# Attention with a forget gate, then a GELU feed-forward layer: another decay and another order in batches 0 and 1

## The chip, the cores and the metric

The kernel runs on one core of one Trainium2 chip. A core has five engines that run their own queues of instructions and wait for each other through semaphores: TensorE (PE in the profile; its weight loads are listed as PEld), VectorE (DVE), ScalarE (ACT), GpSimd (POOL) and SyncE (SP), which only issues transfers. Transfers issued by SP and by POOL go to two different queues, but the same 16 DMA engines carry both. The metric is the device time of one execution in microseconds (us); less is better.

## The reference

There are 8 batches of 8 heads, a sequence of 576 and a head size of 64. `f` is a forget gate between 0.8 and 1. Per head, and then for all 4608 tokens:

```python
scores = scale * np.matmul(q, k.transpose(0, 1, 3, 2))
log_f = np.log(np.clip(f, 0.0001, 1.0))
cum = np.cumsum(log_f, axis=-1)
decay = cum[:, :, :, None] - cum[:, :, None, :]
causal = np.triu(np.ones((S, S), dtype=bool), k=1)
scores = np.where(causal, -1000000000.0, scores + decay)
attn = softmax of scores over the last axis
out = np.matmul(attn, v)
...
x = out of all heads side by side, (4608, 512)
h = x @ w_in                      # 512 -> 2048
y = gelu(h) @ w_out               # 2048 -> 512
```

The decay of query t and key s is the sum of log f over s+1 to t. Whatever depends on the query alone falls out of the softmax, so a key needs only a weight that is proportional to exp(-cum[s]). Up to a factor per head that is also the product of f over all positions after s.

## The kernel before, in words

**Layout.** A head pair i (0 to 3) has its queries and keys transposed in `qT[i]` and `kT[i]`, 64 rows for each of its two heads. The 576 keys are five blocks of 128 (`K0`; the last overlaps the fourth and its first 64 rows are zero). The score tiles of a pair are packed into four tiles t (`STILES`), each with both heads, and `scores` makes one: matmuls into a bank pair `s` (two such buffers), then one exponential on ACT into an `e` tile. The causal mask is either added before the exponential by small matmuls of `after` and `key_of` (where `on_pe` is true), or applied after it by an `affine_select` on POOL (L312). The tiles t=1 use four fixed buffers `e4` whose first 64 columns have to stay zero.

**Weights of the keys.** `wT` holds the key weights of all 64 heads, transposed by TensorE. `weigh_v` multiplies v by them (L269; on VectorE for the first two pairs of batch 0, else on POOL) and from batch 1 on copies the weights themselves beside v (L276), so that `attend` gets numerator and denominator in one run of 15 matmuls a head (L331). `normalize` divides (L344, L345), and the result is transposed into `xT`.

**Feed-forward.** `gemm1` computes 16 blocks of the hidden layer for 512 tokens of a batch (L386), each followed by a GELU on ACT (L406). The remaining 64 tokens of each batch are collected in `tails` by `x_tail` and done at the end. The second GEMM of a batch runs as fill between the attention tiles of the next batch: a generator gives one step at a time and `take(fill, n)` runs n of them. A step "n" is one matmul over 128 rows, a step "r" two matmuls over 64 rows each into two banks, which VectorE adds up.

**Batches 0 to 2.** `first_attention` (batch 0) runs while data are still arriving. `second_attention` (batch 1) has only 16 fill steps, `gemm2_first`: for two of the four row blocks, over the first half of `w_out` (L518). The rest of batch 0's second GEMM is `gemm2_second` (L542) and `PLAN_0`, run in batch 2 together with batch 1's (`gemm2_third`; `FILL_2` says how many steps follow each tile). From batch 2 on all is one pattern (`attention`).

**What sets the order.** The order is written by hand: an engine runs its instructions in the order of the program, and SP's and POOL's transfers are issued in that order too. The order of transfers is kept by small instructions on POOL: `gate` and `behind` (L568, L573) read one element of a tile, so that POOL waits there until that tile has landed, and a `memset` of a column of `v_sb` that the load will overwrite (L152, L623, L797) makes SP's next load wait for POOL. POOL issues q, k, `w_in` and `w_out` (L108, L172, L176); SP issues f, v (L120, five transfers a call), the transposing transfers of q and k from batch 2 on (L236, two halves of the heads, q and k each) and of x (L370), and the outputs. From batch 2 on `untangle` (L250, VectorE) sorts the transposed q and k into `qT` and `kT`; batches 0 and 1 have them transposed by TensorE (`transposes_first`, L208 and L217 to L222).

**PSUM.** Three pools of two buffers: `s` (two banks each), `o` and `m` (one bank each). A tile taken from a pool waits until the tile before it in that buffer has been read.

Of the kernel before, what the change touches and what calls it, by code (L numbers as in the profile page):

```python
# [9 lines left out]
FP32 = mybir.dt.float32  # L10
# [43 lines left out]
def kernel(  # L54
# [100 lines left out]
    e4 = [consts.tile([P, 2, 448], BF16, name=f"e4{i}") for i in range(4)]  # L155
    for t in e4:
        nc.gpsimd.memset(t[:, :, 0:D], 0.0)
    diagonal(ident_fp, Alu.not_equal, 1.0, 0)
    load_qk_tokens(0, 6, 8)
# [20 lines left out]
    ones = consts.tile([BH, S], FP32)  # L180
    lf = f_sb
    cum = consts.tile([BH, S], FP32)
    wk = f_sb
    nc.vector.memset(ones, 1.0)
    nc.vector.memset(wT[0:D, 4, :], 0.0)
    nc.vector.tensor_scalar(f_sb, f_sb, 1e-4, 1.0, Alu.max, Alu.min)
    nc.scalar.activation(lf, f_sb, Act.Ln)
    nc.vector.memset(v_sb[0:D, :, 4, :], 0.0)
    nc.vector.tensor_tensor_scan(cum, ones, lf, 0.0, Alu.mult, Alu.add)
    spark = consts.tile([1, 1], FP32)  # L190
    nc.scalar.activation(spark, ones[0:1, 0:1], Act.Exp)

    def warm_up(n):

        ps = m_psum.tile([P, TC], FP32, tag="m", name="ps_w")
        for _ in range(n):
            nc.tensor.matmul(ps, warm[:, 0:P], warm, start=True, stop=True)
# [82 lines left out]
    def scores(b, i, t):  # L280
        on_pe = b == 0 or (b == 1 and i == 0)
# [170 lines left out]
    PLAN_0 = [(2, "o", 16 * "r"), (3, "m", 14 * "r" + 2 * "n")]  # L452
# [57 lines left out]
    def gemm2_first(c):  # L510

        pss = [
            m_psum.tile([P, d_model], FP32, tag="m", name="ps2") for _ in range(2)
        ]
        for kq in (0, 4):
            for ts in range(2):
                for kt in range(kq, kq + 4):
                    nc.tensor.matmul(  # L518
                        pss[ts],
# [3 lines left out]
                        stop=(kt == 7),  # L523
                    )
                    if kt == 7:
                        ot_of.append(
                            o_pool.tile([P, d_model], FP32, tag="ot", name="ot")
                        )
                        copy = nc.scalar.copy if ts else nc.vector.tensor_copy
                        copy(ot_of[ts], pss[ts])  # L530
                    yield

    def gemm2_second(c):

        for ts, pool, tag in ((0, o_psum, "o"), (1, m_psum, "m")):
# [3 lines left out]
            for kt in range(8, n_ff):  # L539
                for r in range(2):  # L540
                    rows = slice(r * D, (r + 1) * D)
# [4 lines left out]
                        start=(kt == 8),  # L546
                        stop=(kt == n_ff - 1),
                    )
                if kt == n_ff - 1:
                    nc.vector.tensor_tensor(ot_of[ts], ot_of[ts], banks[1], Alu.add)  # L550
                    sum_out(c, ts, ot_of[ts], banks[0])
                yield

    def gemm2_third():
        yield from gemm2_second(0)
        yield from gemm2_rows(0, PLAN_0)
# [18 lines left out]
    def first_attention():  # L575
# [6 lines left out]
        def attend_head(i, h):  # L582
# [5 lines left out]
        nc.scalar.activation(  # L588
            wk, cum, Act.Exp, bias=cum[:, S // 2 : S // 2 + 1], scale=-1.0
        )  # L590
        warm_up(2)
        scores(0, 0, 0)
        scores(0, 0, 1)
        transposes(1, m_psum, "m")
        scores(0, 0, 2)
        psw = o_psum.tile([P, NBLK, BH], FP32, tag="o", name="psw")
        for n in range(NBLK):
            nc.tensor.transpose(
                psw[:, n, :], wk[:, K0[n] : K0[n] + P], ident_fp[:BH, :BH]
# [24 lines left out]
        load_v(1, 0, 4)  # L624
# [6 lines left out]
        for i, t in ((2, 2), (2, 3), (3, 0), (3, 1), (3, 2), (3, 3)):  # L631
            scores(0, i, t)
            attend_head(*heads.pop(0))
# [87 lines left out]
    def second_attention():  # L721
# [23 lines left out]
        transposes(1, o_psum, "o")  # L745
        transposes(2, m_psum, "m")
        transposes(3, o_psum, "o")
        tiles(0, 2)
# [4 lines left out]
        take(fill, 4)  # L753
        weigh_v(1, 2)
# [12 lines left out]
        behind(qk_of[2][1], H - 1)  # L767
        load_w_out(2)
        load_w_out(3)
        run(2)  # L770
        take(fill, 4)
# [74 lines left out]
```

## Time and profile before

| | us |
|---|---|
| median of 5 executions | 338.3 |
| all five | 337.43, 338.23, 338.3, 339.55, 339.72 |
| the profiled execution | 339.55 |
| its span, first to last instruction | 337.6 |
| TensorE busy in it | 328.5 |
| VectorE, ScalarE, GpSimd busy | 181.1, 209.3, 122.2 |
| first attend of batch 0 starts at | 17.0 |
| first GEMM of batch 0 starts at | 25.3 |
| first scores of batch 1 at | 40.9 |
| first scores of batch 2 at | 72.3 |

All times inside the kernel are counted from the start of the span. A line of the timeline or of the groups reads: start and length in us, engine, line of the kernel, operation, the tile written and the tiles read (buffer numbers left out), their shapes, how many instructions are put together, and in brackets how long the engine had been idle before and what ended that. L12 is line 12 of the kernel. "SPq" is a transfer that SP issues; its length is the time of the issue, not of the transfer. The named releaser of a wait is inferred; when the one that is named had long been done, it was another, often a transfer.

### The profile page before, as it was taken

The numbers are of one execution on the slowest core, as the hardware profiler recorded it, in microseconds if no ns is written. First come the engines' busy times: TensorE is split into PE (matmuls) and PEld (weight loads), VectorE is DVE, ScalarE is ACT, GpSimd is POOL, SyncE is SP. The second block draws the span as 40 slices with busy tenths as digits, with TensorE's granted clock in tenths as the row PEclk, the third lists the DMA queues.
The fourth block names the chain that finished last, engine by engine and source line by source line (L and its number), as shares of the span: only waits on it lengthen the run. The fifth ranks groups of instructions, "written<-read, shape, count | busy, mean of one in ns | idle before, by whom it ended". The sixth has DMA issues, their size and how long they took to land.

```text
span 337.6 us, 7820 instructions
## 1 busy us (share of the span) xinstructions
PE 328.5 (97%) x3161; PEld 173.6 (51%) x3161; DVE 181.1 (54%) x414; ACT 209.3 (62%) x299; POOL 122.2 (36%) x250
## 2 busy tenths in 40 slices
PE   8799989999999999999999999999999999999995
PEld 3584455445554456545554465446544654444443
DVE  4661166674556944895479547974696540020011
ACT  6957698673553689278927982788468855404600
POOL 8091088009536135533454254624351420000000
PEclk9979999999999999999999999999999999999999
DMA  7999999996998989697968697679810241011013
GB/s 115 178 142 185 196 196 163 133 201 127 229 211 186 139 156 208 124 140 114 212 163 123 119 208 176 95 121 208 142 62 2 81 61 64 0 63 64 0 39 86
DMA packets 104627, 44.16 MB, mean 131 GB/s; under 512 B 83408, under 2 KB 100048, under 8 KB 104592
## 3 DMA queue, kind: packets, MB, share of 16 engines
q1 hardware_dynamic: 87296, 29.52, 45.7%
q0 software_dynamic: 16896, 13.63, 27.9%
q8 instruction: 24, 0.39, 0.5%
q10 hardware_dynamic: 400, 0.52, 0.4%
q14 instruction: 11, 0.09, 0.1%
HBM read 36.85 MB, written 9.44 MB: 137 GB/s over the span
## 4 chain that ended last, share of the span: by engine, by line
PE 91%; DMA 2%; POOL 1%; DVE 1%; issue 1%; ACT 1%; SPq 0%; POOLq 0%; ACTq 0%; DVEq 0%
PE ps L386 37%; PE ps L482 27%; PE o L331 10%; PE ps L422 8%; PE s L300 7%; DMA v_sb<-in_v_dram 2%; ACT e L310 1%; PE ps L542 1%; POOL q L108 1%; PE ps_x L364 1%; PE ps L518 1%; SPq L120 0%; POOL k L108 0%; DVE qT L217 0%; DVE kT L217 0%
## 5 line engine op out<-in xcount | busy, mean ns | idle before, releaser
L406 ACT ACTIVATE g<-ps 128x512 bf16<-128x512 f32 x144 | 82.1, 601 | 83.6 <-PE ps L386 83.6
L310 ACT ACTIVATE e<-s 128x896 bf16<-128x896 f32 (+2 forms) x128 | 100.3, 835 | 23.1 <-PE s L300 16.8
L386 PE MATMUL ps<-xT,w_in_sb 128*128 128x512 bf16 x512 | 112.5, 379 | 0.0
L482 PE MATMUL ps<-w_out_sb,g 64*128 64x512 bf16 (+1 forms) x711 | 108.3, 377 | 0.0
L386 PEld LDWEIGHTS <-w_in_sb 128*128 128x128 bf16 x576 | 56.0, 98 | 67.5 <-issue 1.8
L312 POOL TENSOR_SCALAR_AFFINE_SELECT e<-e 128x256 bf16<-128x256 bf16 (+1 forms) x135 | 49.1, 383 | 87.9 <-ACT e L310 87.5
L482 PEld LDWEIGHTS <-g 64*128 64x128 bf16 (+1 forms) x711 | 40.5, 95 | 34.3 <-issue 4.5
L269 POOL TENSOR_TENSOR vw<-v_sb,wT 128x640 bf16<-128x640 f32 x30 | 38.5, 1286 | 28.5 <-PE ps L542 15.9
L300 PE MATMUL s<-qT,kT 64*128 64x320 bf16 (+4 forms) x384 | 44.8, 278 | 2.5 <-ACT e L310 1.4
L250 DVE COPY kT<-tk 64x288 bf16<-64x288 bf16 x96 | 45.0, 469 | 1.6
L250 DVE COPY qT<-tq 64x288 bf16<-64x288 bf16 x96 | 37.6, 392 | 5.6 <-DMA tq<-q 4.2
L331 PEld LDWEIGHTS <-e 128*128 128x128 bf16 x960 | 35.2, 99 | 9.5 <-issue 2.8
L331 PE MATMUL o<-vw,e 128*128 128x65 bf16 x960 | 38.2, 196 | 1.3 <-DVE vw L269 1.3
L490 DVE COPY ot<-ps 128x512 f32<-128x512 f32 x20 | 13.8, 692 | 47.2 <-PE ps L482 47.2
L345 DVE TENSOR_TENSOR x<-o,r 128x320 bf16<-128x320 f32 x64 | 31.5, 491 | 2.3
L300 PEld LDWEIGHTS <-kT 64*128 64x128 bf16 x384 | 20.2, 94 | 24.1 <-issue 7.9
L431 DVE COPY ot<-ps 128x512 f32<-128x512 f32 (+2 forms) x9 | 5.7, 632 | 49.6 <-PE ps L422 49.6
L422 PE MATMUL ps<-w_out_sb,g 128*128 128x512 bf16 (+2 forms) x144 | 28.0, 355 | 0.0
L422 PEld LDWEIGHTS <-g 128*128 128x128 bf16 x144 | 13.5, 98 | 14.5
L344 DVE RECIPROCAL r<-o 128x5 f32<-128x5 f32 x64 | 12.1, 189 | 13.4 <-PE o L331 13.3
L502 DVE TENSOR_TENSOR ot<-ot,ps 128x512 f32<-128x512 f32 x22 | 15.1, 685 | 1.1
L386 PE MATMUL ps<-tails,w_in_sb 128*128 128x512 bf16 x64 | 14.3, 377 | 0.0
(69 smaller groups left out, 139.1 us busy)
## 6 DMA issues: line engine op xcount, KB each, us to landing
out_dram<-ot SPq DMA_DIRECT2D x32, 256.0 KB, 2.6
v_sb<-in_v_dram SPq DMA_DIRECT2D x24, 256.0 KB, 4.9
q<-in_q_dram POOLq DMA_DIRECT2D x6, 576.0 KB, 6.4
k<-in_k_dram POOLq DMA_DIRECT2D x6, 576.0 KB, 8.9
v_sb<-in_v_dram SPq DMA_DIRECT2D x22, 128.0 KB, 5.4
w_in_sb<-in_moe_w_in_dram POOLq DMA_DIRECT2D x4, 512.0 KB, 7.7
w_out_sb<-in_moe_w_out_dram POOLq DMA_DIRECT2D x4, 512.0 KB, 10.6
q<-in_q_dram POOLq DMA_DIRECT2D x4, 144.0 KB, 4.7
```

The source lines that it names most:

```text
L250: nc.vector.tensor_copy(rows[:, odd], src[odd * D : (odd + 1) * D, 2 * i + h].rearrange("d j p -> d p j"),)
L269: eng.tensor_tensor(vw(b)[:, hs, :, 0:D], v_sb[:, hs, :, :], w.unsqueeze(3).to_broadcast([P, 2, NBLK, D]), Alu.mult,)
L300: nc.tensor.matmul(to, *ab, start=half < 0, stop=half == 1 or not masked)
L310: nc.scalar.activation(et[:, :, z:c], st[:, :, z:c], Act.Exp, scale=scale)
L312: nc.gpsimd.affine_select(out=et[:, :, c0 + z : c0 + P], in_=et[:, :, c0 + z : c0 + P], compare_op=Alu.is_ge, fill=0.0, base=z, pattern=[[ ...
L331: nc.tensor.matmul(o[:, m, :], e_of[b, i, t][:, h, c : c + P], vw_of[b][:, 2 * i + h, n, :], start=(n == 0), stop=(n == m),)
L345: nc.vector.tensor_tensor(x_of[b, i][:, :, h, :], o[:, :, 0:D], r.unsqueeze(2).to_broadcast([P, NBLK, D]), Alu.mult,)
L386: nc.tensor.matmul(ps, w_in_sb[:, kt, ffb * P : (ffb + 1) * P], src[:, kt, 0:TC], start=(kt == 0), stop=(kt == n_dm - 1),)
L406: nc.scalar.activation(g_of[c][ffb], ps, Act.Gelu)
L422: nc.tensor.matmul(pss[ts][:, c0:c1], g_of[c][kt][:, ts * P : (ts + 1) * P], w_out_sb[:, kt, c0:c1], start=(kt == 0), stop=(kt == n_ff - 1),)
L482: nc.tensor.matmul(banks[r], g_of[c][kt][rows, ts * P : (ts + 1) * P], w_out_sb[rows, kt, :], start=kt == (steps.index("r") if r else 0), ...
L502: nc.vector.tensor_tensor(ot, ot, bank, Alu.add)
```

## The change

The key weights come from a product: `tensor_tensor_scan` on VectorE runs backwards over f, multiplies from 2^80 on, and adds zeros (`none`). The logarithm, the cumulative sum and the exponential of it are gone. The scan stands after the copies of the first pair's keys. The `e4` tiles are zeroed by VectorE and not by POOL, the last loads of q and k of batch 0 come before the mask of `ident_fp`, the second warm-up is two matmuls of 256 columns and not of 512, and the key transposes of pair 1 come after score tile (0, 2).

In batch 0 the last six score tiles are made in twos, followed by two heads' `attend`. In batch 1 pair 3 is masked by TensorE. v of batch 1 arrives in three lots (two, two and four heads), the last two behind the gate on q of batch 1. `gemm2_first` does all four row blocks over the first quarter of `w_out`, and `gemm2_second` all four over the rest. The second quarter of `w_out` is loaded together with the third and fourth, behind the gate on k of batch 2; k of batch 2 is issued later than q, in the middle of batch 1's attention. The fill steps of batch 1 stand at other places.

```diff
-    e4 = [consts.tile([P, 2, 448], BF16, name=f"e4{i}") for i in range(4)]
-    for t in e4:
-        nc.gpsimd.memset(t[:, :, 0:D], 0.0)
+    load_qk_tokens(0, 6, 8)
     diagonal(ident_fp, Alu.not_equal, 1.0, 0)
-    load_qk_tokens(0, 6, 8)
...
-    nc.vector.memset(ones, 1.0)
+    nc.vector.memset(none, 0.0)
+    nc.scalar.activation(spark, none[0:1, 0:1], Act.Exp)
+    nc.vector.memset(v_sb[0:D, :, 4, :], 0.0)
     nc.vector.memset(wT[0:D, 4, :], 0.0)
+    nc.vector.memset(decay[:, S - 1 : S], 2.0**80)
+    e4 = [consts.tile([P, 2, 448], BF16, name=f"e4{i}") for i in range(4)]
+    for t in e4:
+        nc.vector.memset(t[:, :, 0:D], 0.0)
     nc.vector.tensor_scalar(f_sb, f_sb, 1e-4, 1.0, Alu.max, Alu.min)
-    nc.scalar.activation(lf, f_sb, Act.Ln)
-    nc.vector.memset(v_sb[0:D, :, 4, :], 0.0)
-    nc.vector.tensor_tensor_scan(cum, ones, lf, 0.0, Alu.mult, Alu.add)
-    nc.scalar.activation(spark, ones[0:1, 0:1], Act.Exp)
...
-        on_pe = b == 0 or (b == 1 and i == 0)
+        on_pe = b == 0 or (b == 1 and i in (0, HP - 1))
...
-    PLAN_0 = [(2, "o", 16 * "r"), (3, "m", 14 * "r" + 2 * "n")]
...
     def gemm2_first(c):
-        for kq in (0, 4):
-            for ts in range(2):
-                for kt in range(kq, kq + 4):
+        for two in (0, 2):
+            pss = [
+                m_psum.tile([P, d_model], FP32, tag="m", name="ps2") for _ in range(2)
+            ]
+            for ts in (two, two + 1):
+                for kt in range(n_ff // 4):
...
-                        copy = nc.scalar.copy if ts else nc.vector.tensor_copy
+                        copy = nc.scalar.copy if ts == 3 else nc.vector.tensor_copy
...
     def gemm2_second(c):
-        for ts, pool, tag in ((0, o_psum, "o"), (1, m_psum, "m")):
+        kts = range(n_ff // 4, n_ff)
+        for ts in range(n_sub):
+            pool, tag = ((o_psum, "o"), (m_psum, "m"))[ts % 2]
+            steps = "r" * len(kts) if ts < 3 else "r" * (len(kts) - 2) + "nn"
...
     def gemm2_third():
         yield from gemm2_second(0)
-        yield from gemm2_rows(0, PLAN_0)
         yield from gemm2_rows(1, PLAN_1)
...
         transposes(0, o_psum, "o")
-        nc.scalar.activation(
-            wk, cum, Act.Exp, bias=cum[:, S // 2 : S // 2 + 1], scale=-1.0
+        nc.vector.tensor_tensor_scan(
+            decay[:, S - 2 :: -1],
+            f_sb[:, S - 1 : 0 : -1],
+            none[:, 0 : S - 1],
+            2.0**80,
+            Alu.mult,
+            Alu.add,
         )
-        warm_up(2)
+        warm_up(2, 2 * P)
         scores(0, 0, 0)
         scores(0, 0, 1)
-        transposes(1, m_psum, "m")
+        transposes_first(0, 1, 0, m_psum, "m")
         scores(0, 0, 2)
+        transposes_first(0, 1, 1, m_psum, "m")
...
-        load_v(1, 0, 4)
+        load_v(1, 0, 2)
...
-        for i, t in ((2, 2), (2, 3), (3, 0), (3, 1), (3, 2), (3, 3)):
+        for i, t in ((2, 2), (3, 0), (3, 2)):
             scores(0, i, t)
+            scores(0, i, t + 1)
+            attend_head(*heads.pop(0))
             attend_head(*heads.pop(0))
...
         tiles(0, 0)
-        transposes(1, o_psum, "o")
-        transposes(2, m_psum, "m")
+        transposes(1, m_psum, "m")
+        transposes(2, o_psum, "o")
+        take(fill, 2)
+        tiles(0, 2)
         transposes(3, o_psum, "o")
-        tiles(0, 2)
         take(fill, 2)
         tiles(1, 0)
         run(0)
         tiles(1, 2)
         take(fill, 4)
+        load_qk_tokens(2, which="k")
         weigh_v(1, 2)
...
         behind(qk_of[2][1], H - 1)
+        load_w_out(1)
         load_w_out(2)
         load_w_out(3)
         run(2)
-        take(fill, 4)
+        take(fill, 2)
         av(3, 0)
...
                 if ffb == 12:
                     behind(qk_of[1][0], H - 1)
-                    nc.gpsimd.memset(v_sb[:, 4:8, 0, 0:1], 0.0)
+                    nc.gpsimd.memset(v_sb[:, 2:8, 0, 0:1], 0.0)
+                    load_v(1, 2, 4)
                     load_v(1, 4, 8)
                     weigh_v(1, 0)
-                    load_w_out(1)
                     weigh_v(1, 1)
-                    load_qk_tokens(2)
+                    load_qk_tokens(2, which="q")
```

## The prediction

> **What bounds the kernel now.** I read the page first, for the shares.
>
> ```profile
> span 337.6 us, 7820 instructions
> PE 328.5 (97%) x3161; PEld 173.6 (51%) x3161; DVE 181.1 (54%) x414; ACT 209.3 (62%) x299; POOL 122.2 (36%) x250
> PEclk9979999999999999999999999999999999999999
> ```
>
> TensorE is busy nearly all the time, so a part of the change is worth only what it does to TensorE's few holes. The slice line shows one stretch of reduced clock past the start. The table of windows gives it (columns: length; busy time of PE, weight loads, DVE, ACT, POOL; granted clock; DMA share; GB/s):
>
> ```profile
> 10.24:13.66 3.42, 2.69 (x66) 1.96 (x66) 1.93 (x5) 3.36 (x6) 0.00 (x0) 1.00 1.19 216
> 13.66:17.07 3.41, 1.70 (x39) 1.24 (x38) 2.43 (x4) 3.01 (x4) 0.89 (x2) 1.00 0.58 126
> 17.07:20.48 3.41, 3.41 (x53) 2.75 (x53) 2.02 (x5) 0.83 (x2) 3.35 (x4) 0.50 0.62 86
> ```
>
> A window with TensorE 50% busy was followed by half clock, one with 79% was not. Next, the timeline of batch 0:
>
> ```profile
> 16.16 1.56 DVE L269 TENSOR_TENSOR vw<-v_sb,wT 128x640 bf16<-128x640 f32 x2 [0.75 <-DMA v_sb<-in_v_dram]
> 17.04 0.98 PE L331 MATMUL o<-vw,e 128*128 128x65 bf16 x15 [1.35 <-DVE vw L269]
> 18.60 0.70 ACT L310 ACTIVATE e<-s 128x640 bf16<-128x640 f32 x1 [1.91 <-PE s L300]
> ```
>
> The first attend waits for v from HBM, not for the decay, and the scores queued behind it leave ACT idle too. Then the timeline where batch 2 starts, with the queue entries that feed it:
>
> ```profile
> 49.34 0.41 POOL L312 TENSOR_SCALAR_AFFINE_SELECT e<-e 128x256 bf16<-128x256 bf16 x1 [0.19 <-ACT e L310]
> 49.97 1.28 POOL L269 TENSOR_TENSOR vw<-v_sb,wT 128x640 bf16<-128x640 f32 x1 [0.22 <-POOL e L312]
> ...
> 56.50 0.18 POOL L573 CAST gate<-k 96x1 f32<-96x1 bf16 x1
> 56.63 1.56 POOL L176 DMA_DIRECT2D w_out_sb<-in_moe_w_out_dram  x2
> ...
> 75.71 0.69 DVE L502 TENSOR_TENSOR ot<-ot,ps 128x512 f32<-128x512 f32 x1
> ...
> 76.25 1.28 POOL L269 TENSOR_TENSOR vw<-v_sb,wT 128x640 bf16<-128x640 f32 x1 [15.89 <-PE ps L542]
> ...
> 80.61 1.72 POOL L312 TENSOR_SCALAR_AFFINE_SELECT e<-e 128x256 bf16<-128x256 bf16 x5
> ...
> 83.95 1.11 PE L331 MATMUL o<-vw,e 128*128 128x65 bf16 x30
> ```
>
> POOL's 15.89 us is put down to a matmul, but the last v load of batch 2 was issued at 71.36 and took 4.7 us, so it landed at 76.1: v is what POOL waited for. From there POOL works without a gap (two weighings, the q and k issues of batch 3, five masks) until 82.33. The attend that needs the masks starts at 83.95, so v has 1.6 us of slack there. The transfers around it, software queue (q0) and SP's queue (q1), are packets, MB and share, in the stretches 60 to 64, 64 to 68 and 70 to 75 us:
>
> ```profile
> q0 software_dynamic: 348, 0.36, 87.2%
> q1 hardware_dynamic: 224, 0.06, 46.7%
> ...
> q0 software_dynamic: 619, 0.62, 91.1%
> q1 hardware_dynamic: 623, 0.16, 30.7%
> ...
> q1 hardware_dynamic: 4468, 1.13, 134.0%
> ```
>
> While w_out loads, SP's queue gets 156 packets per us (623/4); alone it gets 894 (4468/5). The transposes of q and k and the loads of v for batch 2 all stand in SP's queue behind this.
>
> **The change part by part.**
>
> *Decay and start.* Gone are Ln (0.68 us on ACT), the Exp of the decay (0.77) and one table load (1.28). The scan (1.35, DVE) now runs after the key copy, about 7.1 to 8.4, ahead of the next query copy at 8.51; its reversed reading has no row. Between 1.35 and twice that, the worst delays a key copy by 1.3 us, which the 1.35 us wait for v absorbs. I take 0. ACT's exponentials start 0.1 us earlier, and the first attend still waits for v. The four e4 memsets (0.22 each on POOL; the DVE memset of a similar size took 0.17) go into DVE's idle time before f lands at 3.6. The last q and k loads are issued 0.8 us sooner and share the transfers with v: v lands between 0.3 earlier and 0.3 later; 0. The two smaller warm-up matmuls lie ahead of a copy that TensorE waits for anyway: 0. The later key transposes leave the copy ready at about 10.4, when ACT frees the score bank (10.5): 0, or 0.2 if late.
>
> *Tiles in twos.* Scores (2,3), 0.54 us at half clock (17.95 on), move into the 1.35 us hole. Scores (3,1) now fall into the half-clock window instead and cost 0.3 more. Net -0.25. If the extra 0.45 us (50% to 63% busy) keeps the clock up, the 3.3 us of half-clock work that follows takes about 1.9: another -1.4. The window lies between the two rows above; it is nearer to the throttled one, so I take -0.25. The Trainium skill ("TensorE: Matmul & The Clock Gate", the table of why this matters) warns of idle gaps over about 3 us. This trace throttled after a longest gap of 1.35 us, so the measurement decides; by the rule the clock would play no part and the head would gain 0.25 in any case.
>
> *Batch 1.* The 16 plus 94 matmuls of the early second GEMM are only reordered; VectorE gets two more copies of 0.68, in idle time. Two fill steps (0.43) move from the tail to the front. There they lie beside ACT's stream, which has 0.2 to 0.3 us holes; ACT gains 0.2 and loses as much. Pair 3 gets 18 mask matmuls: a masked and a plain (t=3) tile took 0.33 and 0.32 us, while the mask rows' busy time gives 1.9 per pair (9.5 over five pairs); I take 0.4, since the work is narrow and overlaps. POOL is spared 1.9 us of selects (4 at 0.41, one at 0.29). But the k issue (0.78) now stands between mask (1,3) and weighing (1,2), so the masks of pair 2 end at 55.3 instead of 54.5 and `run(2)`, at 54.79 before, waits until then. With the two fills gone from behind it, the stage ends 0.1 later; bounds -0.4 and +0.6. v in three lots: half of 2304 packets leaves the queue before 39, q and k of batch 1 land 1 to 2 us sooner, and the rest of v lands by about 45 (47 before). w_out's first quarter (43.96 before) lands by about 42.5, just in time for a fill at 42.8. If it lands as before, the fill holds the scores up 1.1, of which ACT's own backlog hides half.
>
> *w_out's second quarter, and k of batch 2.* Its 512 KB leave 43 to 49 and join the other two behind the gate on k. They are 512 packets (619 packets were 0.62 MB); at 155 per us the shared stretch grows 3.3 us. In it q1 still moves 515 packets, worth 0.6 us alone: +2.7 on what stands last, v. k itself is issued at 49.8 (46.13 before, landing 55.8). From the issue, 1.6 us of start, 768 packets at 249 per us alone (1745 in 47 to 54) or 156 beside the q transposes, and 1.5 us to the landing give 56.0 to 57.8; I take 57.1, the middle. The gate opens at 57.1 and not 56.5: +0.6. So v lands 3.3 later, 79.4; POOL's 6.25 us from landing to last mask end at 85.7; the attend moves from 83.95 to about 85.75: **+1.8**. Bounds on v's delay: 1.5 (w_out at the 207 per us that w_in had alone in 20 to 23 us, gate as early as before), which the slack hides, cost 0; and 6.0 (k at 57.8 and one more pause like 62 to 63.5 us), cost +4.4. Beside it, VectorE: the last k transpose is 2 to 3 us later, `untangle` ends near 78, and its two adds (0.69 each) free the o banks at 79.3. The third row block needs them at 78.4, since the first two are 12 steps long now, not 8. That 0.9 us lies inside the 1.8. The last w_out quarter lands at 69.3 + 3.9 = 73.2 and is read at 74.3.
>
> The Trainium skill ("SBUF — State Buffer", the warning on DVE blocking DMA in the section "SBUF: two separate sides") says that VectorE's fast copies keep GpSimd from writing descriptors. Here the q issue at 107.47 took 0.81 us beside such copies, as elsewhere. By the page the third w_out issue, at 58.7, could wait out copies of 0.34 from 59.8, an estimate of under 0.5; by the row, nothing.
>
> **The sum.** The late v sets a time of its own: the small gains ahead (-0.25 + 0.1) only lengthen the wait for it. So +1.8 on the profiled execution's own 339.55 us (span 337.6 and 1.95 around it): 341.35. That execution lies 1.25 above the median; on the median 338.3 it is 340.1. After 84 us TensorE has no hole to give it back.
>
> **The rivals.**
> *The slack holds* (338.2). The transfers have time: the sum of all loads is unchanged, and q0 moved only 33 packets in 56 to 60. Then v is at most 1.6 us late and -0.25 + 0.1 is left. Against it: 60 to 75 us has no room.
> *The clock stays full* (336.4), the other side. Place: 17 to 20.5 us; price -1.4 - 0.25, and -0.3 from batch 1 near its bound. It decides when the window before it is busy enough, somewhere between 50% and 79%, and v of batch 2 keeps its slack because POOL's masks, the k issue and the gate move up with TensorE. Against it: several loads before 44 us run at their own pace.
> *w_out lands last* (343). If the mixed traffic pauses as in 60 to 64 (572 packets against 1242), the last quarter lands at 75 to 77 and TensorE stops at its twelfth step in front of everything else. 1.1 us of slack speaks against it.
> *The product decay changes nothing*: it is off the path whichever rival holds.
>
> **How the numbers follow.** Late v 0.50 (own range 339.3 to 342.2), slack holds 0.23, full clock 0.23, w_out last 0.04. Half a per cent, 1.7 us, is about what a measurement can tell. Of late v 0.07 stays below 340.0, so same is 0.23 + 0.07 = 0.30, slower 0.43 + 0.04 = 0.47, faster 0.23. The range 336.2 to 342.2 takes in the fast case's centre and late v's upper half, and leaves out about 0.1 on either side.
>
> **What would show it.** Right: POOL's first weighing of batch 2 at 79 or later and the first batch 2 attend waiting on POOL; three w_out issues from about 57; ACT without its 1.91 us hole at 16.7. Wrong: that weighing before 78, or no half clock after 17 us. The prediction fails most easily on the pace of the mixed queues, for which there is one stretch of evidence.

## The result: 0.44% slower, and lost in another place than forecast

The changed kernel takes 339.54 us (median of 43 executions) against 338.13 (80 executions of the kernel before): a ratio of 1.0044, 95% interval 1.0031 to 1.0057. The forecast was 340.1 against 338.3. The profiled execution took 340.64 us with a span of 338.7, 1.1 above its median.

Some executions of every kernel here run a few microseconds at a reduced TensorE clock and most of them are 1 to 5 us longer, so where I compare spans below I take those whose mean granted clock was 0.997 or more ("at full clock"): a median of 335.7 for the kernel before (29 of 35 that ran beside the first experiments) and of 337.6 after (37 of all 44).

The head of the page, after:

```profile
span 338.7 us, 7859 instructions
PE 327.8 (97%) x3179; PEld 171.4 (51%) x3179; DVE 183.1 (54%) x421; ACT 206.9 (61%) x296; POOL 119.6 (35%) x241
PEclk9999999999999999999999999999999999999999
```

The shares hardly move: 18 matmuls more, POOL 2.6 us less, and no slice below full clock. The windows that answer to the three shown of before:

```profile
10.24:13.66 3.42, 2.78 (x68) 1.95 (x67) 2.45 (x6) 3.31 (x6) 0.00 (x0) 1.00 1.22 231
13.66:17.07 3.41, 2.80 (x68) 2.15 (x68) 3.10 (x5) 3.38 (x5) 1.63 (x3) 1.00 0.65 136
17.07:20.48 3.41, 3.33 (x88) 2.73 (x86) 2.44 (x8) 2.79 (x5) 2.37 (x3) 1.00 1.08 138
```

One would like to credit the change with the full clock after 17 us. A second profile of the unchanged kernel takes that away; its windows there:

```profile
13.66:17.07 3.41, 2.57 (x59) 1.92 (x59) 3.19 (x6) 2.93 (x4) 1.92 (x4) 1.00 0.62 106
17.07:20.48 3.41, 3.41 (x88) 2.78 (x86) 2.50 (x7) 2.87 (x4) 3.41 (x5) 1.00 1.07 177
```

So the half clock was a chance of the one execution that the forecast was read from (mean clock 0.995). From here on "before" in a comparison of times within the span is this second profile (span 336.0). The start after, in the timeline:

```profile
15.32 1.55 DVE L268 TENSOR_TENSOR vw<-v_sb,wT 128x640 bf16<-128x640 f32 x2
...
16.27 1.12 PE L330 MATMUL o<-vw,e 128*128 128x65 bf16 x30
...
17.90 1.62 ACT L309 ACTIVATE e<-s 128x896 bf16<-128x896 f32 x2 [0.61 <-PE s L299]
```

The 1.35 us hole of TensorE and ACT's 1.91 are not there. But most of both belonged to that one execution as well; in the second profile of before they are 0.51 and 0.50:

```profile
16.12 0.63 PE L331 MATMUL o<-vw,e 128*128 128x65 bf16 x15 [0.51 <-DVE vw L269]
```

The first GEMM of batch 0 starts at 22.75, against 23.08: 0.33 gained. Then batch 1, TensorE and ACT:

```profile
42.15 0.60 PE L516 MATMUL ps<-w_out_sb,g 128*128 128x512 bf16 x2 [1.97 <-DMA w_out_sb<-in_moe_w_out_dram]
43.23 1.51 ACT L309 ACTIVATE e<-s 128x896 bf16<-128x896 f32 x2 [1.48 <-PE s L299]
```

The same wait before, second profile:

```profile
42.89 0.39 PE L518 MATMUL ps<-w_out_sb,g 128*128 128x512 bf16 x1 [0.51 <-DMA w_out_sb<-in_moe_w_out_dram]
```

The early fill step waits 1.97 us for w_out's first quarter, and the score tiles queued behind it starve ACT for 1.48. The first GEMM of batch 1 starts at 56.65, against 55.88. POOL's line of work after:

```profile
55.20 0.18 POOL L575 CAST gate<-k 96x1 f32<-96x1 bf16 x1 [1.41 <-DMA k<-in_k_dram]
55.43 2.32 POOL L173 DMA_DIRECT2D w_out_sb<-in_moe_w_out_dram  x3
...
77.07 1.28 POOL L268 TENSOR_TENSOR vw<-v_sb,wT 128x640 bf16<-128x640 f32 x1 [17.91 <-PE ps L544]
...
79.81 0.84 POOL L108 DMA_DIRECT2D q<-in_q_dram  x1
```

and before, second profile:

```profile
55.43 1.57 POOL L176 DMA_DIRECT2D w_out_sb<-in_moe_w_out_dram  x2
73.41 1.28 POOL L269 TENSOR_TENSOR vw<-v_sb,wT 128x640 bf16<-128x640 f32 x1 [15.02 <-DMA v_sb<-in_v_dram]
...
76.16 0.84 POOL L108 DMA_DIRECT2D q<-in_q_dram  x1
```

The gate is passed at 55.2 in both and the issues behind it begin at the same 55.43, three in place of two, and v of batch 2 is weighed 3.66 us later; q and k of batch 3, which stand behind that weighing on POOL, are issued 3.65 later. Why v is late shows in the queues in the stretch of 64 to 68 us (packets, MB, share), after:

```profile
q0 software_dynamic: 624, 0.62, 91.4%
q1 hardware_dynamic: 624, 0.16, 29.9%
```

The same stretch before, second profile:

```profile
q1 hardware_dynamic: 2978, 0.75, 96.9%
q0 software_dynamic: 209, 0.20, 29.2%
```

With w_out under way SP's queue gets 156 packets per us (624/4), one for each packet of the software queue; before, w_out was nearly done by then. The attend of batch 2 pays for this only 0.5: its two heads start at 82.57 and 83.52, against 81.81 and 82.28. The larger price comes 20 us later. TensorE at the first GEMM of batch 2:

```profile
102.98 1.06 PE L385 MATMUL ps<-xT,w_in_sb 128*128 128x512 bf16 x4
105.27 2.97 PE L385 MATMUL ps<-xT,w_in_sb 128*128 128x512 bf16 x13 [1.22 <-DMA xT<-x]
```

and before, second profile, where it runs through:

```profile
101.75 6.42 PE L386 MATMUL ps<-xT,w_in_sb 128*128 128x512 bf16 x29
```

What it waits for, the last transposes of x, come late out of SP's queue. SP's queue in the timeline after:

```profile
86.67 8.11 SPq L120 DMA_DIRECT2D v_sb<-in_v_dram  x5
...
102.58 2.56 SPq L369 DMA_TRANSPOSE xT<-x  x2
```

The same two steps before, second profile:

```profile
85.70 5.03 SPq L120 DMA_DIRECT2D v_sb<-in_v_dram  x5
...
97.78 2.55 SPq L370 DMA_TRANSPOSE xT<-x  x2
```

SP spends 8.1 us on the issues of v for batch 3, not 5.0, while q and k of batch 3 are loading: k lands at 92.25 (11.6 us after its issue), and before at 86.06 (9.1), when SP had only begun. The x transposes stand behind these issues. Milestone by milestone, after less before: scores of batch 1 −0.28; first GEMM of batch 1 +0.77; scores of batch 2 +0.76; second attend head of batch 2 +1.24; scores of batch 3 +2.65; end +2.7. That is one profile against one; at full clock the medians differ by 1.9, the profiled execution after being one of the longer ones.

### The profile page after: what moved, and what is told of

Read it like the earlier page. It is cut to its first block, busy times and chain, and to the rows that moved or that the text cites. A ratio compares the mean times of both kernels' runs of the same rounds, so it can differ in the third digit from the quotient of the medians.

```text
span 338.7 us, 7859 instructions
## 1 busy us (share of the span) xinstructions
PE 327.8 (97%) x3179; PEld 171.4 (51%) x3179; DVE 183.1 (54%) x421; ACT 206.9 (61%) x296; POOL 119.6 (35%) x241
## 4 chain that ended last, share of the span: by engine, by line
PE 83%; DMA 7%; POOL 3%; ACT 2%; DVE 1%; issue 1%; SPq 1%; ACTq 0%
PE ps L385 32%; PE ps L480 23%; PE ps L421 8%; PE o L330 8%; PE s L299 7%; DMA w_out_sb<-in_moe_w_out_dram 5%; ACT e L309 2%; DMA xT<-x 2%; PE ps L544 2%; PE ps_w L194 1%; POOL vw L268 1%; PE ps L516 1%; PE ps_f L207 1%; POOL q L108 1%; POOL k L108 1%
## 5 line engine op out<-in xcount | busy, mean ns | idle before, releaser
L480 PE MATMUL ps<-w_out_sb,g 64*128 64x512 bf16 (+1 forms) x649 | 100.4, 377 | 0.0
L311 POOL TENSOR_SCALAR_AFFINE_SELECT e<-e 128x256 bf16<-128x256 bf16 (+1 forms) x130 | 47.2, 383 | 83.2 <-ACT e L309 83.0
L480 PEld LDWEIGHTS <-g 64*128 64x128 bf16 (+1 forms) x649 | 36.4, 95 | 31.3 <-issue 3.8
L249 DVE COPY kT<-tk 64x288 bf16<-64x288 bf16 x96 | 44.1, 459 | 4.0 <-DMA tk<-k 2.5
L299 PE MATMUL s<-qT,kT 64*128 64x320 bf16 (+4 forms) x384 | 44.0, 276 | 2.2 <-ACT e L309 1.4
L249 DVE COPY qT<-tq 64x288 bf16<-64x288 bf16 x96 | 39.0, 406 | 4.1 <-DMA tq<-q 2.7
L330 PEld LDWEIGHTS <-e 128*128 128x128 bf16 x960 | 34.3, 98 | 8.3 <-POOL e L311 2.9
L330 PE MATMUL o<-vw,e 128*128 128x65 bf16 x960 | 37.3, 194 | 0.1
L488 DVE COPY ot<-ps 128x512 f32<-128x512 f32 x18 | 12.4, 691 | 44.3 <-PE ps L480 44.3
```

Source lines behind the costliest of these rows:

```text
L249: nc.vector.tensor_copy(rows[:, odd], src[odd * D : (odd + 1) * D, 2 * i + h].rearrange("d j p -> d p j"),)
L299: nc.tensor.matmul(to, *ab, start=half < 0, stop=half == 1 or not masked)
L311: nc.gpsimd.affine_select(out=et[:, :, c0 + z : c0 + P], in_=et[:, :, c0 + z : c0 + P], compare_op=Alu.is_ge, fill=0.0, base=z, pattern=[[ ...
L330: nc.tensor.matmul(o[:, m, :], e_of[b, i, t][:, h, c : c + P], vw_of[b][:, 2 * i + h, n, :], start=(n == 0), stop=(n == m),)
L480: nc.tensor.matmul(banks[r], g_of[c][kt][rows, ts * P : (ts + 1) * P], w_out_sb[rows, kt, :], start=kt == (steps.index("r") if r else 0), ...
```

## The experiments

All times are in us. "Span" is the median of the executions at full clock, and how many those were; "v" is how long after the first scores of batch 2 POOL begins to weigh v; "xT" is the wait of the first GEMM of batch 2; "batch 1" is what TensorE waits there for POOL's masks (P) or for w_out (W). The last three are from one profile each.

| run | edit | ratio to before, interval | span | batch 1 | v | xT |
|---|---|---|---|---|---|---|
| e0 | the kernel before again | 0.9997 [0.9976, 1.0018] | 335.8 (11 of 12) | W 0.5 | 3.1 | 0 |
| the change | | 1.0044 [1.0031, 1.0057] | 337.6 (37 of 44) | W 2.0 | 6.0 | 1.2 |
| e1 | w_out's 2nd quarter early | 1.0057 [1.0029, 1.0086] | 337.8 (9 of 12) | P 0.5+0.7 | 5.4 | 1.0 |
| e2 | fill later | 1.0017 [0.9993, 1.0041] | 337.5 (12 of 12) | none | 6.2 | 1.2 |
| e3 | head alone | 0.9999 [0.9970, 1.0028] | 335.7 (10 of 12) | W 1.4, k 1.2 | 3.7 | 0 |
| e4 | both moves undone | 1.0094 [1.0058, 1.0129] | none at full clock | P 1.4+0.7 | 1.6 | 0 |
| e5 | e4 and fill later | 1.0075 [1.0039, 1.0111] | 337.2 (3 of 12) | (none) | (0.7) | 0 |
| e6 | e5 with POOL's masks | 1.0066 [1.0036, 1.0096] | 337.6 (4 of 12) | P 2.6+0.7 | 2.2 | 0 |
| e7 | e2, v of batch 3 later | 1.0287 [1.0242, 1.0333] | none at full clock | none | 5.8 | 0 |
| f1 | e5, v in two lots | 1.0009 [0.9975, 1.0042] | 335.7 (8 of 12) | (none) | (−2.0) | 0 |
| f2 | e2, v in two lots | 1.0054 [1.0017, 1.0091] | 338.2 (10 of 12) | none | 5.8 | 1.2 |
| f3 | e2, k with q | 1.0029 [1.0000, 1.0058] | 337.4 (10 of 12) | P 0.5 | 5.9 | 0.2 |
| g1 | f1 with the early fill | 1.0116 [1.0097, 1.0135] | 336.5 (1), 340.2 (1) of 7 | W 2.1 | 1.1 | 0 |

The values in brackets are from profiles with half clock from about 7 to 24 us, where compute comes 4 to 6 us later than the loads.

**e0, the kernel before again.** No edit.

> The kernel before, unchanged, for a second profile and the granted clock of several executions. If the half-clock window after 17 us belongs to the kernel before, most executions show a mean clock near 0.995 and the first GEMM of batch 0 starts at 25.3 us. If it was the chance of one execution, most show 0.998 or more, the first GEMM starts about 1.4 us sooner, and the head of the changed kernel is worth that much less than the two profiles suggest.

It was chance: full clock, the first GEMM at 23.08. In six of the 35 executions of before that ran beside it the mean clock was under 0.997.

**e1, w_out's second quarter early.**

```
-        load_w_out(1)
...
                     weigh_v(1, 0)
+                    load_w_out(1)
                     weigh_v(1, 1)
```

> The changed kernel with the second quarter of w_out issued where the kernel before issues it. Theory 'late queue' (the quarter behind the gate on k delays v of batch 2, q and k of batch 3 and SP's queue, and the x transposes of batch 2 come late): v of batch 2 lands before 75, the 1.2 us wait of the first GEMM of batch 2 for a transposed x is gone, and the time falls by 1.2 to 1.5 us from the changed kernel's, to about 338.1. Rival 'early fill' (the loss is the 2.0 us wait of the first fill step for the first quarter of w_out): no change, 339.5.

Nothing was gained, so the theory "late queue" failed in this form. v came 0.7 us sooner against its scores, and batch 1 got a new wait: the second lot of v of batch 1 shares the transfers with that quarter, POOL weighs it at 44.8 (42.45 before, 43.98 with the change), its masks are late, and the attend at 47 us waits 0.47 and 0.70.

**e2, fill later.**

```
-        take(fill, 2)
         tiles(0, 2)
         transposes(3, o_psum, "o")
-        take(fill, 2)
+        take(fill, 4)
```

> The changed kernel with the first two fill steps of batch 1 behind score tiles (0, 2) and (0, 3) and the transposes of pair 3, where the kernel before has them. 'Early fill': the 2.0 us wait of TensorE is gone, ACT's exponentials of batch 1 follow each other, the first scores of batch 2 come 1.0 to 1.5 us sooner (at about 69.8) and the time falls to about 338.2. 'Late queue': the batch 2 scores come sooner but the wait on the x transposes grows by as much, and the time stays 339.5.

The wait of 1.97 is gone and the scores of batch 2 start at 70.31 (70.29 before, 71.05 with the change). The end hardly moves: a span of 337.5 against 337.6, a median of 339.37 us against 339.54. (The ratio in the table is lower than that of the change, but the intervals overlap.) The wait for xT is as long as with the change:

```profile
104.69 3.61 PE L385 MATMUL ps<-xT,w_in_sb 128*128 128x512 bf16 x16 [1.20 <-DMA xT<-x]
```

The forecast had said that small gains ahead only lengthen a later wait. In this profile the wait is no longer, and 0.58 of the 0.74 gained is still there at the scores of batch 3 (117.73 against 118.31); that the medians don't show it is not explained.

**e3, the head alone** (the product decay, tiles in twos and the start's order, in the kernel before; the rest as before).

> The kernel before with the part of the change in batch 0 alone: product decay, e4 zeroed by VectorE, the earlier q and k loads, score tiles in twos. If the head carries to the end, the first GEMM of batch 0 starts near 22.8 and the time is 335.5 to 336.7. If batch 1 runs at the pace of its loads (v of batch 1 landed at 41.6, the first quarter of w_out at 44.0 in the profile before), the head's gain is waited away there and the time is 337.7 to 338.2.

The head brings 0.16 to the first GEMM (22.92 against 23.08, one profile each) and none to the end. In this profile it is taken back in batch 1, where TensorE waits for loads:

```profile
41.31 0.45 PE L207 MATMUL ps_f<-key_of,k 96*64 96x96 bf16 x12 [1.17 <-DMA k<-in_k_dram]
44.24 0.39 PE L517 MATMUL ps<-w_out_sb,g 128*128 128x512 bf16 x1 [1.38 <-DMA w_out_sb<-in_moe_w_out_dram]
```

**e4, both moves of transfers undone** (e1, and k of batch 2 issued with q).

```
                     weigh_v(1, 0)
+                    load_w_out(1)
                     weigh_v(1, 1)
-                    load_qk_tokens(2, which="q")
+                    load_qk_tokens(2)
```

> The changed kernel with both moves of transfers of batch 1 undone: the second quarter of w_out is issued where it was (behind the first weighing of batch 1), and k of batch 2 together with q behind the gate's place of before. The theory 'late queue' (what costs is that v of batch 2, and with it the issue of q and k of batch 3, come 3 us later, and that the x transposes of batch 2 then wait): v of batch 2 lands by 74.5 us, q of batch 3 is issued by 77.5, the first GEMM of batch 2 no longer waits 1.0 to 1.2 us for xT; what is left is the fill that waits for the first quarter of w_out (1.0) less the head (0.3): about 338.5 against 338.0. The rival 'batch 1 alone' (the cost lies in the reordered second GEMM and the masks on TensorE): 339.4 as the changed kernel.

The late part went as the theory "late queue" said: v 1.6 us after its scores, no wait for xT, and nothing lost behind batch 1 (first GEMM of batch 1 3.1 later than before, end of span 3.2 later). But the forecast of 338.5 failed, at 341.06. The loss is all in batch 1, 3.1 us where the waits for POOL add up to 2.1. TensorE there:

```profile
48.70 0.24 PE L330 MATMUL o<-vw,e 128*128 128x65 bf16 x2 [1.40 <-POOL e L311]
49.64 1.91 PE L330 MATMUL o<-vw,e 128*128 128x65 bf16 x28 [0.71 <-POOL e L311]
```

The windows there (length; busy time of PE, weight loads, DVE, ACT, POOL; granted clock; DMA share; GB/s):

```profile
47.80:51.20 3.40, 1.79 (x28) 1.50 (x29) 0.40 (x2) 1.05 (x2) 3.40 (x8) 0.75 0.97 131
51.20:54.60 3.40, 3.40 (x41) 1.60 (x39) 1.66 (x4) 1.95 (x3) 3.21 (x8) 0.75 1.31 202
```

The clock is at half from 49.52 to 52.93, which gives 0.75 in both windows. In the 3.42 us ahead of that, 46.10 to 49.52, TensorE was busy 1.44 us. So the two waits cost their own 2.1 us and some of the clock behind them.

**e5, e4 and the fill later.**

> The same, and the two early fill steps of batch 1 behind score tiles (0,2) as well. What is left of the change is the head, v of batch 1 in three lots, the second GEMM that begins with one quarter of w_out, and the masks of the last pair on TensorE. 'Late queue' and 'early fill' together account for the whole cost: 337.4 to 338.0, the span at or under that of the kernel before. If the masks on TensorE or the reordered GEMM cost something: 338.5 or more.

"Together account for the whole cost" failed: the median is 340.69 us, only 3 of 12 executions are at full clock, and their span is 337.2, 1.5 above that of before. The cost had to be in what was left.

**e6, as e5, with POOL's masks for the last pair.**

```
-        on_pe = b == 0 or (b == 1 and i in (0, HP - 1))
+        on_pe = b == 0 or (b == 1 and i == 0)
```

> As the run with loads and fill undone, but the last pair of batch 1 masked by POOL as before. TensorE has 18 narrow matmuls less (0.4 us by the prediction), POOL 1.9 us of selects more, ahead of the gate. If the masks lie on TensorE's path and POOL has time: 0.4 faster than that run. If POOL is what batch 1 waits for: its gate and w_out issues 1 to 2 us later, v of batch 2 too, and 0 to 1 us slower.

The ratio is that of e5 (1.0066 against 1.0075): giving the masks back to POOL gains nothing. The 0.4 us of the 18 mask matmuls alone would be too little to see, since the intervals are 0.3% (1 us) to either side. Its profile has the longest of the waits for POOL in batch 1, and its windows show what follows:

```profile
47.80:51.20 3.40, 0.35 (x5) 0.23 (x5) 0.03 (x1) 1.32 (x2) 3.39 (x9) 1.00 0.46 53
51.20:54.60 3.40, 3.32 (x35) 1.91 (x34) 1.38 (x4) 1.10 (x2) 3.40 (x7) 0.56 1.29 199
```

POOL weighs v's second lot at 46.70 there, after 6.65 us of waiting for it; with v in two lots (g1) it does at 42.19.

**e7, v of batch 3 behind the transposes of its k** (and the fill later).

```
-                    if b == 2 and i == 1:
-                        load_v(3)
...
             transpose_dma(3, 4, 8)
+            load_v(3)
```

> The changed kernel with the early fill steps behind score tiles (0,2), as in the run 'fill later', and v of batch 3 issued on SP's queue behind the transposes of k of batch 3, not ahead of the transposes of x of batch 2. The transfers of w_out and k stay as the change has them, so v of batch 2 stays late (76 us). The theory 'SP order' (the late queue costs by x transposes of batch 2 that stand behind v of batch 3): the wait of the first GEMM of batch 2 for xT (1.2 us in 'fill later') is gone or under 0.3, about 338.1. The rival (q and k of batch 3 on the other queue slow the x transposes whatever stands ahead of them): the wait stays at 1 or more, 339.4.

In its place the theory "SP order" is right: the x transposes are in time, although v of batch 2 is as late as ever, and the first GEMM of batch 2 runs through from 101.75, as before. As a remedy it fails, by 2.9%, and by the same chain one batch on. POOL now waits for v of batch 3 until 112.74 and issues q and k of batch 4 behind it at 117.34 (105.15 before). Their transposes stand in SP's queue ahead of those of x, which SP issues from 138.29 on (130.77 before), and the first GEMM of batch 3 waits. TensorE in that place:

```profile
141.14 0.59 PE L385 MATMUL ps<-xT,w_in_sb 128*128 128x512 bf16 x1 [4.26 <-DMA xT<-x]
143.06 3.18 PE L385 MATMUL ps<-xT,w_in_sb 128*128 128x512 bf16 x7 [1.33 <-DMA xT<-x]
```

The windows there, the nearly idle one first:

```profile
136.58:140.00 3.42, 0.30 (x2) 0.02 (x1) 0.00 (x0) 0.00 (x0) 1.45 (x2) 1.00 1.22 190
140.00:143.40 3.40, 0.93 (x2) 0.21 (x2) 2.18 (x5) 0.00 (x0) 0.00 (x0) 0.53 0.77 183
143.40:146.80 3.40, 3.40 (x9) 1.14 (x8) 3.24 (x11) 0.00 (x0) 1.00 (x2) 0.50 0.77 219
```

**f1, e5 with v of batch 1 in two lots.**

```
-        load_v(1, 0, 2)
+        load_v(1, 0, 4)
...
-                    load_v(1, 2, 4)
                     load_v(1, 4, 8)
```

> As the run with loads and fill as before, but v of batch 1 in two lots again (heads 0 to 3 before w_out, heads 4 to 7 behind the gate). What is left of the change is the head, the second GEMM that begins with one quarter of w_out, and the masks of the last pair on TensorE. Theory 'lots need the empty queue' (with v in three lots, POOL's second weighing of batch 1 waits for a load that shares the engines with w_out's second quarter; undoing the move of w_out alone therefore made it worse): that weighing starts before 42.5 us, the attend at 47 us no longer waits 1.4 to 2.6 us for POOL, no half clock follows, and the time is 337.4 to 338.1; the first fill may wait up to 1.4 us for w_out as it did with the head alone. Rival 'masks and order of the second GEMM': still a wait or more work on TensorE before 58 us, 338.8 or more.

335.7 at full clock, as before the change; five of these eight executions are at 335.4 to 335.7, the others at 337.3 to 340.0. What is left in it, the head, the second GEMM that begins with one quarter and the masks on TensorE, costs and brings nothing that can be measured: 1.0009, with an interval of 0.34% to either side. So, by the spans, the cost of the change lies in the three things that f1 undoes, the early fill, the two moves and the three lots (the intervals of the two ratios still overlap, up to 1.0042 and from 1.0031). (f1's profiled execution had half clock in the start, so its batch 1 is no evidence, and that v comes early enough there isn't either.)

**f2, both moves, two lots.** The edit of f1 in e2.

> The changed kernel with the early fill steps behind score tiles (0,2) and v of batch 1 in two lots: the two moves of transfers (w_out's second quarter and k of batch 2) stay. With the runs 'fill later' (moves and three lots), 'loads and fill' (three lots alone) and 'two lots' (neither) it makes a table of two by two. Theory 'moves': v of batch 2 stays late (75.5 to 76.5 us) and the first GEMM of batch 2 waits 1.0 to 1.2 us for xT: 338.8 to 339.4. Rival 'lots' (the lots and not the moves cost): v of batch 2 by 74.5, no such wait, 338.1.

The theory "moves" holds in its sign: the wait for xT is 1.17 as in e2 (v itself was weighed at 75.56 as it said, the time is 340.26 and not under 339.4). With e2, e5 and f1 this is the table of two by two, spans at full clock: neither 335.7, three lots alone 337.2 (three executions only), moves alone 338.2, both 337.5. By these, each of the two costs 1.5 to 2.5 by itself. (The intervals of the ratios of f1 and f2 overlap; the reading rests on the spans and on the wait for xT, which f1's profile doesn't have and f2's has.) Together they cost less than their sum. A reason can be seen, though no run isolates it: the moves clear w_out's second quarter out of the way of v's later lots, so that the second lot is weighed at 43.39 in e2, and at 44.80 in e1 and 46.70 in e6, where the quarter is early.

**f3, k with q.**

```
-        load_qk_tokens(2, which="k")
...
-                    load_qk_tokens(2, which="q")
+                    load_qk_tokens(2)
```

> The changed kernel with the early fill steps behind score tiles (0,2), and k of batch 2 issued together with q (as before), while w_out's second quarter stays behind the gate. k no longer has w_out's second quarter ahead of it in the queue and should land 1.5 to 3 us earlier than in 'fill later' (54.1); the gate then opens at 52.5 to 53.5 and not at 54.4, and the three quarters of w_out end as much earlier. If v of batch 2 is late only because w_out starts late: v by 75 us, q of batch 3 by 78, the wait for xT under 0.4, 337.9 to 338.4. If three quarters in one block are too long whenever they start: v after 75.7, wait of 1, 339.3. POOL's masks of pair 0 come 0.8 us later by the issue of k; if the attend at 47 us waits for them, 0.5 to 1 more.

k did not land sooner (the gate opened at 54.65, 54.19 in e2), so the way to an earlier w_out wasn't opened, and v came at 76.83. The span is that of e2 within 0.1. So undoing k's move alone gains nothing. That what the two moves cost hangs on w_out's quarter is not shown: no run undid that one alone with v in two lots, and with three lots (e1) it gained nothing either. The wait for xT is nearly gone (0.21); in its place the second head of batch 1's second attend comes 1.0 later than in e2, behind POOL's masks (a wait of 0.45), and the stages of batch 2 lose 0.3 and 0.4 to before. The loss is in other places and its sum is the same.

**g1, f1 with the early fill.** The two fill steps ahead of `tiles(0, 2)`, as the change has them.

> As the run 'two lots' (both moves of transfers and the three lots undone), but with the two early fill steps ahead of score tiles (0,2), where the change has them. In 'fill later' the early fill seemed to cost only 0.2 us of the whole, because the late queue took the gain back at the x transposes of batch 2. If that is so, it costs in full here, where the queue is in time: TensorE waits 1.5 to 3 us for w_out's first quarter near 40 to 42 us, ACT's backlog hides about half, and the span in undisturbed executions is 0.7 to 1.5 over that of 'two lots' (335.7), so 336.4 to 337.2; v of batch 2 lands by 74.5 us and the first GEMM of batch 2 doesn't wait for xT. If the early fill is really cheap (0.2): 335.7 to 336.0.

The profiled execution is as expected: a wait of 2.07 us for w_out, a span of 336.5, 0.8 over f1, v 1.1 after its scores and no wait for xT. That agrees with an early fill that costs in full where the queue is in time, and that the late queue had hidden; one execution can't show it. The other six executions have spans of 339.6 to 340.2, five of them with clocks of 0.98 to 0.993 and one at 1.00. No profile shows them; what adds 3 us there is open, and with it what the early fill costs by itself.

## Why the prediction was right, and where not

**The time** came out close (339.5 against 340.1), in part by luck. The late v of batch 2 was there as forecast. The place where it is paid was another, batch 1 lost 1.05 that was priced at 0.1, and the three lots, which cost something by themselves too (e5), were counted as a small gain.

**Decay and start, 0; tiles in twos, −0.25.** Right in size: −0.33 to the first GEMM with the whole change, −0.16 with the head alone (e3). But the hole that it was worked out from was 0.51 and not 1.35 in the second profile. None of it reaches the end.

**The clock (−1.4 more, and the rival at 336.4).** Wrong, though it needed no run to be seen in part. The half clock from 17 us belonged to one execution; 29 of the 35 beside it had a mean clock of 0.997 or more. Having taken the profiled execution's 1.25 above the median off the sum, the rival then took the same microseconds off again as a gain. Against the median there was nothing to win but the 0.25.

**Batch 1, +0.1 (−0.4 to +0.6).** It measured +1.05 (from −0.28 at the first scores to +0.77 at the first GEMM). The step that failed is "w_out's first quarter lands by about 42.5, just in time for a fill at 42.8". The landing was right, 42.10. The fill was ready at 40.18, since without the half clock the scores of batch 1 start 2.3 us earlier (38.59 against 40.86) while the quarter lands only 1.1 earlier (42.84 against 43.96). The "if" of that paragraph, a stop of 1.1 with half of it hidden, was the right mechanism; the stop measured 1.97. The 18 mask matmuls (0.4) are too small to be seen in e6.

**The gate, +0.6.** Wrong: it was passed at 55.2 in both profiles. k, issued 3.9 us later, landed at the same 55.15. Why is open. That it no longer stands behind w_out's second quarter can't be all, since in f3, with no such quarter ahead of it and issued 1.45 earlier than in e2, it landed no earlier. (The middle of the two estimates for it, 56.0 and 57.8, is also 56.9 and not 57.1, and the parts named for the upper bound on v's delay, 1.3 for k, 2.7 and a pause of 1.5, make 5.5 and not 6.0.)

**w_out's second quarter, v 3.3 us later.** Right in mechanism: 156 packets per us for SP's queue in the mixed stretch (155 was used). The stretch cost v about 2.4 (its packets run at full rate to 74.85, to 72.45 before) where 2.7 was counted. v is weighed 3.66 later all the same, because some 1.3 come from the end of its transfer, where one packet of another queue lies (the last section). So the 3.3 came near by chance: the gate's 0.6 was missing, and the 1.3 had not been counted. The Trainium skill ("DMA: Bandwidth & Descriptors", the section on queues, rings and completion order) says that a DMA engine takes turns between its queues packet by packet; the 624 and 624 packets of 64 to 68 us agree with that. SP's packets were the smaller (0.16 MB against 0.62), so its queue got the smaller part of the bytes. Unfortunate was the mark "79 or later" for the weighing, with "before 78" as the sign of being wrong: it was set in the time of the disturbed execution, and the weighing came at 77.07, late by about the amount forecast.

**The attend of batch 2 moves by 1.8.** Wrong place: it moves by 0.5 over what was lost ahead. In the second profile of before, the slack between POOL's last mask (79.49) and the attend (81.81) is 2.3 and not the 1.6 counted. The step that failed is "after 84 us TensorE has no hole", taken as if nothing later hung on v. POOL issues q and k of batch 3 right behind the weighing. The forecast listed these issues as part of the 6.25 us to the masks and did not follow them as transfers: 3.65 later, they load beside v of batch 3, SP's queue behind it falls back by 5 us (the x transposes at 100.62 and 102.58, against 95.58 and 97.78), and TensorE gets its hole of 1.22 at 104 to 105 us. e7 shows the same chain once more, with q and k 12.2 late. The stage from there to the scores of batch 3 loses 1.4. By chance 0.5 and 1.4 make about the 1.8.

**The rivals.** "The slack holds" fell with the 3.66. "w_out lands last" did not happen: the last quarter landed at 69.07, and no matmul of batch 2's second GEMM waits for it. Whether VectorE's copies hold up a w_out issue was not tested: the three issues were over at 57.75, and the copies began at 58.18.

**Shown, argued, open.** Shown: the head costs nothing that can be measured (e3, whose interval lies below that of the change); three lots without the moves cost (f1 against e5, just clear of the noise); undoing k's move alone changes nothing (f3 against e2); the xT wait hangs on SP's order (e7). Shown by the spans alone, with ratios whose intervals overlap: the early fill, the moves and the three lots hold the whole cost (f1 against the change), and the two moves cost (f1 against f2). Argued: that in e5 at full clock the price is POOL's wait; its profile has none, e4 and e6 have it. Open: the slower executions of g1, the share of each of the three in the 1.9 us, and what sets k's landing.

No run beat the kernel before. Of the orders of the loads between 36 and 76 us that were tried, none did better than its own.

## What to carry to other kernels

Follow a late transfer to everything that its consumer's engine issues next, the DMAs above all: what is paid at the first reader can be small, and the rest comes two stages later in another queue. Where compute and loads run at different paces, a profile of one execution with a reduced clock can show false slack (w_out's quarter, read 0.6 after its landing in one profile of before and waited for in the other); profile the kernel twice before pricing a wait of a microsecond. And a step moved earlier has to be tested against the landing of what it reads in the fastest execution, not in the one at hand.

## What was not expected of the hardware

**A wait can cost twice, but not always.** In these traces the granted clock falls to half for stretches of 3.41 us or a multiple of that: from 17.07 in the first profile of before, 49.52 in e4, 51.58 in e6 (one each), 140.22 in e7 (two). In the 3.41 us ahead of each, TensorE was busy 1.70, 1.44, 0.65 and 0.08 us. With 2.34 and 2.19 (the change, 41.08 to 44.49 and 102.52 to 105.93) the clock stayed full. The busy share alone does not decide, though. e3 kept the full clock with 1.90 (42.45 to 45.87), while in the starts of e5 and f1 stretches with 2.40 and 2.26 were followed by half clock, which then held for 13.7 and 17.1 us although TensorE was busy 3.41 of 3.41 us in the first stretch of it. The Trainium skill ("TensorE: Matmul & The Clock Gate", the states of the clock gate in part 1) has the clock go to half after at least one idle window of some 3.4 us. e7 and nearly e6 agree; in before and e4 the time ahead was busy to 50% and 42%, with no wait longer than 1.40, so here the measurement goes further than the rule. How often it happens depends on the kernel: none of the executions of e4 and e7 were at full clock, all twelve of e2 were.

**One code packet on one DMA engine.** While v of batch 2 loads, one packet of the instruction queue comes in between. The transfers of 72 to 78 us after, in slices of 0.15 us, and that queue's line:

```profile
DMA  9999999999999999999300000000000002999940
GB/s 222 222 215 215 218 220 217 215 218 222 217 218 326 205 205 197 210 222 218 58 0 3 9 10 9 10 12 19 17 2 0 0 0 96 355 382 382 396 137 0
...
q8 instruction: 1, 0.02, 1.4%
```

At 74.85 nearly all engines are done (9 to 19 GB/s is about a sixteenth of the 220 before), and the rest of v takes until 76.4. The packet began at 73.94 and took 1.3 us. Such a packet of 0.9 to 1.3 us comes near this place in all fourteen profiles, both of before included. In the six where it began while v's packets were still running (the change, e1, e2, e7, f2, f3) the transfer ends in a tail of 1.4 to 1.5 us at that low rate; in the other eight they were through by then, or within 0.1 us of it (e0: packet at 73.05, v's packets through at 72.45), and there is no tail. So v pays in a step: 2.4 late by the shared stretch, its transfer still ran when a packet came that it used to be ahead of. That the tail is the engine which carries the packet is argued from the times; the trace doesn't name the engine.
